# Transposed q copied apart by ScalarE in a retention kernel with a matmul MLP, and another order of its first loads

## The chip, the cores and the metric

The kernel runs on one core of a Trainium2 chip. The metric is the device time of one execution in microseconds (us); lower is better. The kernel before the change took 300.82 us, the median of three runs (300.07, 300.82 and 302.81).

TensorE does the matmuls. VectorE, ScalarE and GpSimd do elementwise work. GpSimd and SyncE also issue the DMA transfers that bring data in and out. Each engine works through its own list of instructions in the order in which the program was written for it; between engines there are only waits on semaphores.

## The reference

```python
# q, k, v: (8 batches, 8 heads, 576 positions, 64); float32
scores = scale * q @ k^T                        # scale = 1/8
Dmat   = gamma[h] ** (i - j) where i >= j else 0
att    = (scores * Dmat) @ v
x      = att.transpose(0, 2, 1, 3).reshape(4608, 512)
h      = x @ w_in                               # w_in: 512 x 2048
out    = 0.5 * h * (1 + erf(h / sqrt(2))) @ w_out   # w_out: 2048 x 512
```

It is an attention with a decay that depends on the head in place of a softmax, and a two-layer MLP with exact GELU over the 4608 tokens that come out of it.

## The kernel before

**Units.** A unit is 128 positions of one batch with all eight heads (or the last 64 positions of two batches, a short unit). Two batches go together as a pair `bp`. Units are collected in groups: groups 0 to 3 are single units, groups 4 to 7 are three pairs and a short unit that TensorE transposes, and groups 8 and up (`BY_DVE`) are 11 pairs and 3 short units. Four units make a block of 512 tokens; the nine blocks go through the MLP one after another.

**Per group.** q and k are loaded (L266 to L317), transposed so that the head dimension lies on partitions, and multiplied to scores (`scores`, L441). VectorE multiplies by the decay mask (`masked`, L490). `inner` (L525) multiplies by v, `state` (L550) makes the 64x64 sum of k times v that later chunks need, and `cross` (L596) adds what q takes from the state of the chunk before it. `evacuate` writes the x tile for the MLP.

**Groups from 8 on.** VectorE transposes 32x32 blocks of 4-byte words (L432). Such a word is a pair of neighbouring bf16 values of the head dimension, so the two numbers of a pair, `y` = 0 and 1, stay side by side in the result. `scores` and `cross` run once for `y` = 0 and once for `y` = 1: for each of four pairs of heads and each `y` four matmuls of 32 rows run in four bands of rows of the array, which is 32 matmuls for a group (L464, L615). q is the operand that streams through. For a pair of units its tokens are read by `turned_q` as (b, u, t) while they lie in memory as (u, b, t, y): two tokens 4 bytes apart, then a jump of 256 bytes to the other half, and back. For a short unit it is an even step of 4 bytes. k is the weight, read with an even step of 4 bytes (`turned_k`).

**MLP.** Block 0 and 1 and blocks 2 to 5 use plain matmuls for the first layer (L658). The last three use a seven-product scheme (`mlp1_fast`, L867), and the second layer uses such a scheme almost throughout (`mlp2_fast`, L762). ScalarE does GELU (L663, L666, L872).

**Who decides the order.** The kernel is one Python loop (L1112 on) that keeps an estimate of every engine's time (`T`), of the landing of loads (`land`) and of free PSUM banks, and writes down next what by those estimates can go next. This is a plan made while the program is built. An entry that a time in the plan delays is only written later into its engine's list; on the chip nothing waits for that time. `fire` (L1045) writes GpSimd's loads in the order of the string `ORDER` (L322), SyncE's loads of v (`load_v`, L257) and the output stores (`put`, L1072).

**Loads.** GpSimd's loads convert to bf16 while they copy. SyncE loads v for the groups from 8 on as float32 in four buffers with the tag `v32`; two of these hold constants at first (`zeros`, `far`), two are free from the start. q and k of a group share one tile with the tag `qk` (four buffers).

Of the kernel before, what the change touches and what calls it, by code (L numbers as in the profile page):

```python
# [17 lines left out]
def kernel(  # L18
# [51 lines left out]
    N_LD = 4  # L70
    N_QKT = 4
# [6 lines left out]
    RATE = 3.8  # L78
    STATE10 = 24.0
# [54 lines left out]
    near = ld_pool.tile([128, 2, HP, 128], FP32, tag="qk", bufs=N_LD, name="near")  # L134
# [21 lines left out]
    def constants():  # L156
# [7 lines left out]
        for h in range(H):  # L164
            nc.scalar.activation(near[:, h % 2, h // 2], far[:, 0, :], AF.Exp, scale=log_gamma[h], bias=ln_scale)
# [64 lines left out]
    def qk_tile(name):  # L230
        return ld_pool.tile([128, 4 * H * D], BF16, tag="qk", bufs=N_LD, name=name)

# [3 lines left out]
    def tiles_of(i):  # L236
        g = groups[group_of[i]]
        if i not in loaded:
            if i < 4:
                loaded[i] = (early_slice(2 * i, 2).rearrange("p (a h d) -> p a h d", a=2, h=H),  # L240
                             early_slice(8 + i, 1).rearrange("p (h d) -> p h d", h=H), None)
            else:
                n = group_of[i]
                if i != g[0]:
                    qk, kn = loaded[i - 1][0], loaded[i - 1][2]
                elif n not in BY_DVE:
                    qk = qk_tile("qk_ld").rearrange("p (a h j d) -> p a h j d", a=2, h=H, j=2)
                    kn = qk[:, 1]
                else:
                    qk = qk_tile("qkb_ld").rearrange("p (a f) -> p a f", a=2)  # L250
                    kn = ld_pool.tile([128, H, 2, D], BF16, tag="kn", bufs=N_KN, name="kn_ld") if len(g) > 1 else None
                loaded[i] = (qk, None if group_of[i] in BY_DVE else ld_pool.tile([128, H, D], BF16, tag="v", bufs=8, name="v_ld"), kn)
        return loaded[i]

    v32 = {}

    def load_v(i):  # L257
# [5 lines left out]
        sw[0] = max(sw[0], T["pe"]) + 0.8  # L263
        land["v", i] = max(T["pe"] + 3.5, sw[0] + 2.0)

    def load(what, i):  # L266
# [25 lines left out]
        if what in "qk" and group_of[i] in BY_DVE:  # L292
# [3 lines left out]
            for jj in (j,) if j is not None else range(2):  # L296
                for e in range(2):
                    p0 = 64 * e + 32 * jj
                    nc.gpsimd.dma_start(qk[p0:p0 + 32, "qk".index(what), 0:HP * per].rearrange("p (h x) -> p h x", h=HP),  # L299
# [10 lines left out]
        for jj in (j,) if j is not None else range(2):  # L310
# [3 lines left out]
            else:  # L314
                dst = qk[:, "qk".index(what)] if i < 4 else qk[0:n, "qk".index(what), :, jj]
# [5 lines left out]
    cast_due = {("q", 0): (loaded[0][0][:, 0], first["q32"]), ("k", 0): (loaded[0][0][:, 1], first["k32"])}  # L321
    ORDER = ("wi0 io k1 q1 v0 k2 wi1 q2 v1 v2 q3 wi4 k3 wi2 v3 wi6 wo0 wi7 wo2 wi3 wi5 wo3 wo1 wo6 wo4 wo5 wo7 k4 "  # L322
             "q5 q4 k5 q6 v4 k6 v5 q7 k7 q8 k8 q9 v7 v8 v6 k9 v9 dq2 q10 dq3 q11 k12 q12 k10 n11 k11 dq4 v10 n12 "
# [70 lines left out]
    def qkT_of(n):  # L394
        s = sg[n]
        if "qkT" not in s:
            if n < 4:
                s["qkT"] = ld_pool.tile([128, 2, HP, 128], BF16, tag="kn", bufs=N_KN, name="qkT")
            else:
                s["qkT"] = tr_pool.tile([128, 2, H, 128], BF16, tag="qkT", bufs=N_QKT, name="qkT")  # L400
        return s["qkT"]

    def turn(n, jj, half):
        qk, qkT = loaded[groups[n][0]][0], qkT_of(n)
        b, t = bank([128, HP, 128], BF16, "qk_ps")
        rows = TAIL if units[groups[n][0]][2] is None else C
        for x in range(HP):
            what = qk[:, jj, 2 * x:2 * x + 2, :] if n < 4 else qk[0:rows, jj, HP * half + x, :, :]
            nc.tensor.transpose(t[:, x, 0:rows], what, ident[0:rows, 0, 0:rows])
        done = pe(0.225)  # L410
        done = either(0.42, 0.6, done, qkT[:, jj, HP * half:HP * half + HP, 0:rows], t[:, :, 0:rows])
# [3 lines left out]
    def turned(n, x):  # L415


        us = 1 if units[groups[n][0]][2] is None else 2
        t = qkT_of(n)[:, x].rearrange("p h s -> p (h s)")[:, 0:HP * us * 128]
        return us, t.rearrange("p (h u b t y) -> p h u b t y", h=HP, u=us, t=2, y=2)  # L420

    def turn_dve(n, x):

        us, t = turned(n, x)
        m = HP * us * 64
        src = loaded[groups[n][0]][0][:, x, 0:2 * m].bitcast(FP32).rearrange("p (h t e) -> p h t e", h=HP, e=32)
        dst = qkT_of(n)[:, x].rearrange("p h s -> p (h s)")[:, 0:2 * m].bitcast(FP32)
        if us == 1 or x == 0:
            src, dst = src.rearrange("p h (u t) e -> p (h u) t e", u=us), dst.rearrange("p (h b t) -> p h t b", t=2, b=32)
        else:  # L430
            src, dst = src.rearrange("p h (t u) e -> p h t u e", u=us), dst.rearrange("p (h u b t) -> p h t u b", h=HP, t=2, b=32)
        nc.vector.transpose(dst, src)  # L432
        sg[n]["T"] = on("dve", 0.13 + m / 960, max(land["qk"[x], i] for i in groups[n])) + SEM

    def turned_q(n, sl, hp, y):
        return turned(n, 0)[1][sl, hp, :, :, :, y].rearrange("p u b t -> p b u t")

    def turned_k(n, sl, hp, y):
        return turned(n, 1)[1][sl, hp, :, :, :, y].rearrange("p u b t -> p (u b t)")

    def scores(n):  # L441
        g = groups[n]
        qkT = sg[n]["qkT"]
        if n < 4:
            got = [bank([128, HP, 128], FP32, "sc") for _ in range(2)]
            for hp in range(HP):
                for e in range(2):
                    sl = slice(64 * e, 64 * e + 64)
                    nc.tensor.matmul(got[e][1][:, hp, :], lhsT=qkT[sl, 1, hp, :], rhs=qkT[sl, 0, hp, :],
                                     start=True, stop=True)  # L450
            st[g[0]]["sc"] = got, pe(0.23, "row")
        elif n in BY_DVE:
# [13 lines left out]
            done = pe(0.27 if short else 0.5, "row4x2" if short else "row4")  # L466
            for j, i in enumerate(g):
                st[i]["sc"] = got if short else got[j], done
        elif len(g) == 1:
            got = [bank([128, H, TAIL], FP32, "sc") for _ in range(2)]  # L470
            for h in range(H):
                for j in range(2):
                    sl = slice(64 * j, 64 * j + 64)
                    nc.tensor.matmul(got[j][1][sl, h, :], lhsT=qkT[sl, 1, h, :TAIL], rhs=qkT[sl, 0, h, :TAIL],
                                     start=True, stop=True)
            st[g[0]]["sc"] = got, pe(0.23, "quad")
        else:
            got = [[bank([128, HP, 128], FP32, "sc") for _ in range(2)] for _ in g]
            for h in range(H):
                for j in range(2):  # L480
                    sl = slice(64 * j, 64 * j + 64)
                    nc.tensor.matmul(got[j][h % 2][1][:, h // 2, :], lhsT=qkT[sl, 1, h, :], rhs=qkT[sl, 0, h, :],
# [7 lines left out]
    def masked(i):  # L490
# [8 lines left out]
        for e in range(2):  # L499
# [6 lines left out]
            else:  # L506
                r = ret_pool.tile([128, HP, 128], BF16, tag=f"ret{e}", name=f"ret{e}")
                by = near[:, e] if i in raw else (mskp if group_of[i] in BY_DVE else msk).to_broadcast([128, HP, 128])
# [41 lines left out]
    def state(bp, ci):  # L550
        pair = pair_of[bp, ci]
        b, u_ps = bank([128, H, D], FP32, "u_ps")
        for hp in range(HP) if packed(pair[0]) else ():
            for y in range(2):
                for e in range(2):
                    for j, i in enumerate(pair):
                        h, p0 = 2 * hp + e, 64 * e + 32 * j
                        keys = loaded[i][0][:, 1, h, y::2] if i < 4 else loaded[i][2][:, h, j, y::2]
# [676 lines left out]
```

## Time and profile before

| | us |
|---|---|
| median of three runs | 300.82 (300.07 to 302.81) |
| the profiled execution | 299.79 |
| its span, first to last instruction | 298.0 |
| TensorE busy | 286.5 |
| VectorE busy | 230.0 |
| GpSimd busy | 152.1 |
| ScalarE busy | 134.3 |

The granted TensorE clock was 1.000 over the span. The profiled execution is 1.79 us longer than its span and 1.03 us shorter than the median. In a line of the profile a group is named by the source line, the engine, the operation and the tiles it writes and reads; the number after `x` counts instructions. Matmuls overlap in the pipeline, and each record lasts until its modelled end, so the time that a run of matmuls costs is read from its start to the start of what follows, not from its busy time. A few per cent of matmul records are missing.

### The profile page before, as it was taken

To read this page: it belongs to the slowest core of one execution; us is meant where nothing else is said; L and a number is where in the kernel's file an instruction comes from. 1 tells how busy PE (TensorE), PEld (TensorE's weight loads), DVE (VectorE), ACT (ScalarE), POOL (GpSimd) and SP (SyncE) were. 2 spreads that over 40 slices of the span, in tenths; PEclk is the share of its full clock that TensorE was granted. 3 is DMA by queue.
4 is the path that set the end of the run, shared out by engine and by line. 5 is a ranking of instruction groups with operands and counts; after the bars stand their busy time and mean duration, and the time that the engine had idled before them with its cause. 6 is when DMAs were issued, how large, how long until landed. Compare 5 with 4: busy or idle time off the path is not lost.

```text
span 298.0 us, 8850 instructions
## 1 busy us (share of the span) xinstructions
PE 286.5 (96%) x3717; PEld 216.2 (73%) x3741; DVE 230.0 (77%) x443; ACT 134.3 (45%) x260; POOL 152.1 (51%) x232
## 2 busy tenths in 40 slices
PE   7999997989999999999999999999999999999994
PEld 2578586868756667666666666666888888888883
DVE  5871795899989899425976789756998999899761
ACT  7456234545254243544342433533554554546521
POOL 8976689879866998999998933000000000000000
PEclk9999999999999999999999999999999999999999
DMA  9999999999999999999999861201102101201013
GB/s 143 167 189 202 184 186 180 194 159 105 143 169 154 169 164 184 147 102 167 216 151 190 72 175 34 70 2 37 37 0 74 70 2 70 73 0 73 35 55 124
DMA packets 112119, 34.79 MB, mean 117 GB/s; under 512 B 89808, under 2 KB 107728, under 8 KB 112080
## 3 DMA queue, kind: packets, MB, share of 16 engines
q0 software_dynamic: 78048, 17.71, 66.8%
q1 hardware_dynamic: 32992, 16.26, 20.7%
q8 instruction: 29, 0.48, 0.7%
q10 hardware_dynamic: 1040, 0.26, 0.4%
q14 instruction: 10, 0.08, 0.1%
HBM read 42.47 MB, written 9.44 MB: 174 GB/s over the span
## 4 chain that ended last, share of the span: by engine, by line
PE 46%; POOL 24%; DMA 21%; issue 4%; DVE 3%; ACT 1%; POOLq 0%
PE fa L762 13%; POOL qkb_ld L299 12%; PE fb L762 10%; DMA kn_ld<-in_k_dram 9%; PE hT L658 7%; PE ha L867 7%; DMA qk_ld<-in_k_dram 6%; PE hb L867 5%; POOL kn_ld L306 5%; DMA w_in<-in_moe_w_in_dram 3%; POOL early L316 3%; DMA v_ld<-in_v_dram 2%; POOL w_in L271 2%; PE o_ps L615 1%; DVE s L730 1%
## 5 line engine op out<-in xcount | busy, mean ns | idle before, releaser
L658 PE MATMUL hT<-x,w_in 128*128 128x512 bf16 (+2 forms) x522 | 92.2, 314 | 1.9 <-ACT x L377 0.4
L658 PEld LDWEIGHTS <-w_in 128*128 128x128 bf16 x544 | 49.4, 98 | 25.0 <-issue 1.9
L762 PEld LDWEIGHTS <-g_all 128*128 128x128 bf16 x544 | 52.4, 98 | 11.8 <-issue 1.1
L663 ACT ACTIVATE g_all<-hT 128x512 bf16<-128x512 f32 x64 | 38.2, 597 | 46.6 <-PE hT L658 44.0
L762 PEld LDWEIGHTS <-s 128*128 128x128 bf16 x408 | 39.4, 98 | 8.9 <-DVE s L730 0.7
L748 DVE TENSOR_TENSOR o_sb<-fb,t 128x256 f32<-128x256 f32 x51 | 21.2, 417 | 22.9 <-PE fb L762 10.0
L872 ACT ACTIVATE g_all<-tt 128x512 bf16<-128x512 f32 x36 | 22.6, 630 | 29.4 <-DVE tt L880 29.3
L762 PE MATMUL fa<-w_out,g_all 128*128 128x256 bf16 x272 | 35.1, 273 | 0.0
L299 POOL DMA_DIRECT2D qkb_ld<-in_k_dram x56 | 30.5, 569 | 5.4 <-DMA kn_ld<-in_k_dram 4.6
L299 POOL DMA_DIRECT2D qkb_ld<-in_q_dram x56 | 30.9, 575 | 4.1 <-DVE ret L509 2.2
L306 POOL DMA_DIRECT2D kn_ld<-in_k_dram x44 | 30.3, 716 | 4.3 <-DMA qkb_ld<-in_q_dram 1.9
L509 DVE TENSOR_TENSOR ret<-sc,mskp 128x512 bf16<-128x512 f32 x44 | 27.2, 677 | 3.0 <-PE sc L464 3.0
L880 DVE TENSOR_TENSOR tt<-hb,tt 128x512 f32<-128x512 f32 x36 | 24.5, 687 | 5.2 <-ACT tt L377 2.9
L377 ACT COPY t<-fa 128x256 f32<-128x256 f32 x38 | 14.1, 372 | 30.4 <-PE fa L762 30.4
L666 ACT ACTIVATE g_all<-hT 128x512 bf16<-128x512 f32 (+1 forms) x36 | 19.3, 552 | 12.5 <-PE hT L658 12.5
L638 DVE TENSOR_TENSOR x<-o_ps,dqT 128x512 bf16<-128x512 f32 (+1 forms) x36 | 20.9, 620 | 1.5 <-PE o_ps L615 1.3
L867 PEld LDWEIGHTS <-ws 128*128 128x128 bf16 x192 | 18.8, 98 | 2.2
L762 PE MATMUL fa<-wt,s 128*128 128x256 bf16 x136 | 17.5, 273 | 0.2 <-DVE s L730 0.2
L762 PE MATMUL fa<-wt,g_all 128*128 128x256 bf16 x136 | 17.5, 273 | 0.2 <-ACT t L377 0.2
L762 PE MATMUL fb<-w_out,g_all 128*128 128x256 bf16 x136 | 17.6, 273 | 0.0
L762 PE MATMUL fb<-wt,s 128*128 128x256 bf16 x136 | 17.5, 273 | 0.0
L762 PE MATMUL fb<-w_out,s 128*128 128x256 bf16 x136 | 17.5, 273 | 0.0
(122 smaller groups left out, 436.3 us busy)
## 6 DMA issues: line engine op xcount, KB each, us to landing
out_dram<-o_sb SPq DMA_DIRECT2D x31, 256.0 KB, 2.3
v<-in_v_dram SPq DMA_DIRECT2D x50, 128.0 KB, 5.5
qkb_ld<-in_q_dram POOLq DMA_DIRECT2D x44, 64.0 KB, 4.0
qkb_ld<-in_k_dram POOLq DMA_DIRECT2D x44, 64.0 KB, 4.3
kn_ld<-in_k_dram POOLq DMA_DIRECT2D x44, 64.0 KB, 4.1
w_in<-in_moe_w_in_dram POOLq DMA_DIRECT2D x8, 256.0 KB, 6.7
w_out<-in_moe_w_out_dram POOLq DMA_DIRECT2D x8, 256.0 KB, 9.8
out_dram<-o_sb SPq DMA_DIRECT2D x8, 128.0 KB, 2.3
```

The costliest lines, as they stand in the source:

```text
L299: nc.gpsimd.dma_start(qk[p0:p0 + 32, "qk".index(what), 0:HP * per].rearrange("p (h x) -> p h x", h=HP), {"q": q, "k": k}[what][2 * bp + jj ...
L306: nc.gpsimd.dma_start(kn[64 * e:64 * e + 64, :, j], k[2 * bp + j, :, ci * C + e:ci * C + C:2, :].rearrange("h s d -> s h d"))
L509: nc.vector.tensor_tensor(r, t, by, op=ALU.mult)
L638: nc.vector.tensor_tensor(x[:, :, n * y:n * y + n], o, dqT[:, :, ci * C:ci * C + n], op=ALU.mult)
L658: nc.tensor.matmul(hT[:, m - m0, :], lhsT=w_in[:, cc, m * 128:m * 128 + 128], rhs=x_tiles[t][:, cc, lo:hi], start=(cc == 0), stop=(cc == N ...
L663: nc.scalar.activation(g_all[:, t % 2, :, m0, :], hT.rearrange("p n (a c) -> p (n a) c", a=2), AF.Gelu)
L666: nc.scalar.activation(g_of(t, 2 * lo // TOK)[:, m0:m0 + n, lo_:lo_ + hi - lo], hT, AF.Gelu)
L748: nc.vector.tensor_tensor(dst, src, f[key], op=ALU.add)
L762: nc.tensor.matmul(dst, lhsT=x[:, kk, :], rhs=y[:, kk, :], start=(name in "125" and kk == 0), stop=(kk == HK - 1), skip_group_check=True)
L867: nc.tensor.matmul(dst[:, m, :], lhsT=a[:, cc, c0:c0 + 128], rhs=y[:, cc, :], start=(name in "125" and m == 0 and cc == 0), stop=(cc == HC ...
L872: nc.scalar.activation(g_of(t, part)[:, m0:m0 + 2], src, AF.Gelu)
L880: nc.vector.tensor_tensor(f[key], f["b"][1], f[key], op=ALU.add)
```

## The change

1. **q apart.** VectorE still transposes q as 4-byte pairs, now into a tile `pairs`, with the tokens in their natural order. A new ScalarE copy (`apart`) then writes the two halves of the pairs, first all `y` = 0 and then all `y` = 1, back into the tile that q was loaded into. `turned_q` becomes a contiguous slice of it. k is left as it was.
2. **Tiles.** q and k have tiles of their own: six for q (`lq`), four for k (`lk`). The q tile is now in use until `cross` has read it. Temporaries and sums of the seven-product scheme move to these tiles; their number and work stay.
3. **Plan.** Durations assumed for scores and cross are shorter. A new `share` adds the cost of SyncE's transfers to the estimated landings of others. Stores of block 0 are written no earlier than a planned 60 us (`STORE_AT`), loads of v no earlier than a planned 58 us (`V_AT`).
4. **Order.** `ORDER` is another string.

```diff
+    N_LQ = 6
+    N_LK = 4
+    N_TQ = 2
+    N_TK = 4
+    STORE_AT = 60.0
+    V_AT = 58.0
+    CROWD = 66.0
...
-    ORDER = ("wi0 io k1 q1 v0 k2 wi1 q2 v1 v2 q3 wi4 k3 wi2 v3 wi6 wo0 wi7 wo2 wi3 wi5 wo3 wo1 wo6 wo4 wo5 wo7 k4 "
-             "q5 q4 k5 q6 v4 k6 v5 q7 k7 q8 k8 q9 v7 v8 v6 k9 v9 dq2 q10 dq3 q11 k12 q12 k10 n11 k11 dq4 v10 n12 "
+    ORDER = ("wi0 io k1 v1 q1 k3 v0 q2 k2 q3 wi1 v2 wi5 wi7 v3 wo4 wi6 wi4 wi2 wo2 wo1 wi3 wo0 wo3 wo7 wo5 wo6 k4 "
+             "q4 q5 k5 v4 k6 q6 v5 q7 k7 v8 q8 dq2 k8 q9 v6 v7 k9 v9 dq3 q11 k12 q10 q12 k10 n11 dq4 k11 n12 v10 "
...
+    def apart():
+        n, ready = apart_due.pop(0)
+        m = pairs_of(n)
+        nc.scalar.copy(loaded[groups[n][0]][0][0][:, 0:2 * m].rearrange("p (y n) -> p y n", y=2),
+                       sg[n]["pairs"].rearrange("p h s -> p (h s)")[:, 0:2 * m].rearrange("p (n y) -> p y n", y=2))
+        sg[n]["T"] = max(sg[n].get("T", 0.0), on("act", 0.15 + m / 580, ready) + SEM)
...
     def turned_q(n, sl, hp, y):
-        return turned(n, 0)[1][sl, hp, :, :, :, y].rearrange("p u b t -> p b u t")
+        m = pairs_of(n)
+        return loaded[groups[n][0]][0][0][sl, y * m + hp * m // HP:y * m + (hp + 1) * m // HP]
...
-        while v_due and v_due[0] < nV + N_V32 and v_due[0] <= nA + V_LEAD and ("q", v_due[0]) in land:
+        while v_due and now > V_AT and v_due[0] < nV + N_V32 and v_due[0] <= nA + V_LEAD and ("q", v_due[0]) in land:
             load_v(v_due.pop(0))
...
+        while apart_due and apart_due[0][1] <= now + 0.1 and T["act"] <= now + (0.5 if apart_due[0][0] > group_of[min(nA, N_U - 1)] else 3.0):
+            apart()
...
-        while stores and stores[0][0] <= now + 0.2:
+        while stores and max(stores[0][0], STORE_AT if stores[0][1] == 0 else 0.0) <= now + 0.2:
             put()
```

In the built programs SyncE's list begins so (the numbers in names tell buffers apart; each `v` entry is two loads of 128 KB):

```
before: load q, 4 stores of block 0, then v 1041, 1203, 1251, 1383, 1532, 1550, 2 stores, ...
after:  load q, v 1192, 1195, then 4 stores of block 0, then v 1245, 1493, 1514, 1532, 2 stores, ...
```

The loads of v 1192 and 1195 wait for no semaphore. GpSimd's list has the same instructions in another order. TensorE's list has two more warming matmuls (23 in place of 21), and ScalarE's has 14 more copies: 11 of 128x1024 and 3 of 128x512 elements.

## The prediction

> **What bounds the kernel.** I read the stages first.
>
> ```profile
> 0.00:15.00 15.00, 13.24 (x110) 5.97 (x112) 10.54 (x43) 9.15 (x22) 13.86 (x22) 1.00 1.63 155
> 15.00:36.00 21.00, 20.52 (x237) 15.85 (x237) 10.51 (x22) 11.24 (x23) 14.33 (x19) 1.00 1.52 193
> 36.00:66.00 30.00, 27.02 (x421) 22.02 (x420) 25.13 (x45) 13.80 (x27) 25.60 (x37) 1.00 2.01 181
> 66.00:120.00 54.00, 53.51 (x875) 37.30 (x880) 50.37 (x91) 21.94 (x41) 44.64 (x77) 1.00 1.24 154
> 120.00:205.00 85.00, 83.30 (x1277) 56.37 (x1291) 56.32 (x103) 34.60 (x66) 53.65 (x81) 1.00 0.78 115
> 205.00:294.00 89.00, 88.91 (x807) 78.72 (x805) 76.75 (x145) 43.61 (x81) 0.00 (x0) 1.00 0.14 47
> ```
>
> Columns: stage, length, busy us of TensorE, its weight loads, VectorE, ScalarE, GpSimd, then clock, DMA share and GB/s. From 66 to 294 us TensorE is busy 225.7 of 228 us, so a microsecond less of matmul there comes off the end. The chain of waits runs over loads up to about 145 us, but TensorE has other work queued meanwhile. Only before 66 us does it stand still for data; the timeline shows where, and how long blocks of small matmuls take.
>
> ```profile
> 49.08 0.61 PE L409 MATMUL qk_ps<-ident,qk_ld 128*128 128x128 bf16 x8 [1.49 <-DMA qk_ld<-in_q_dram]
> ...
> 51.36 0.62 PE L482 MATMUL sc<-qkT 64*128 64x128 bf16 x16
> 51.92 2.79 PE L658 MATMUL hT<-x,w_in 128*128 128x256 bf16 x24
> ...
> 57.35 0.62 PE L482 MATMUL sc<-qkT 64*128 64x128 bf16 x16
> 57.81 0.28 PE L409 MATMUL qk_ps<-ident,qk_ld 64*128 64x64 bf16 x4
> ...
> 62.28 0.39 PE L409 MATMUL qk_ps<-ident,qk_ld 64*128 64x64 bf16 x8 [1.47 <-DMA qk_ld<-in_k_dram]
> ...
> 158.14 0.42 PE L559 MATMUL u_ps<-vh,kn_ld 128*32 128x64 bf16 x32
> 158.49 0.85 PE L615 MATMUL o_ps<-qkT,u_sb 32*64 32x128 bf16 x32
> 159.27 0.84 PE L464 MATMUL sc<-qkT 32*128 32x128 bf16 x32
> 160.04 1.05 PE L762 MATMUL fb<-w_out,g_all 128*128 128x256 bf16 x8
> ```
>
> From start to start cross (L615) takes 0.78 us and scores (L464) 0.77: eight steps of four parallel matmuls over 128 tokens, and the single starts lie 84 ns apart. L482 also makes eight steps over 128 tokens (two parallel matmuls each), but reads q contiguously: 0.56 us, starts 56 ns apart.
>
> **The contiguous q.** There are 11 full score blocks and 9 full cross blocks (352/32 and 288/32 in the groups). At L482's 0.56 each saves 0.22: 20 x 0.22 = 4.4 us. That the jumps cause the 84 ns, and not the four bands, is read from the short blocks: same four bands, 64 tokens in an even step of 4 bytes, 32 ns per step; twice that is 64, not 84. It also gives the low bound, since k as weight keeps its 4-byte step: 64 ns a step saves 8 x 20 ns = 0.16 a block, 3.2 us in all. High bound: 0.46, the L482 block at 57.35 that runs straight into the next, 0.32 x 20 = 6.4. I take 4.4, because L482 is followed by the same change of mode. The six short blocks take 0.38; 32 contiguous matmuls of 64 columns take 0.35 (158.14 to 158.49): 6 x 0.03 = 0.2. Sum **-4.6** (-3.4 to -6.6).
>
> [...]
>
> **ScalarE's copies.** They are new, in a list that GELU shares.
>
> ```profile
> L377 ACT COPY t<-fa 128x256 f32<-128x256 f32 x38 | 14.1, 372 | 30.4 <-PE fa L762 30.4
> L377 ACT COPY tt<-ha 128x512 f32<-128x512 f32 x17 | 9.6, 579 | 3.3 <-PE ha L867 3.2
> L576 ACT CAST u_sb<-u_acc 128x512 bf16<-128x512 f32 x8 | 4.9, 618 | 13.4 <-DVE u_acc L574 13.4
> ```
>
> From 256 to 512 elements a copy grows by 0.21 us; 1024 then take 0.58 + 2 x 0.21 = 1.0, which is an estimate from these rows. Eleven of these and three of 512 make 12.7 us. Between 66 and 205 us ScalarE works 56.5 of 139 us, so they fit. Behind a copy in the list stand GELUs and PSUM evacuations, and TensorE waits for those through its eight banks. The cover is shown by L576: eight times ScalarE stood, 13.4 us in all, for VectorE, while the idle time of TensorE that its copies to u_acc (L571) ended is 0.4 us in the group of L658. I put **+0.4** (0 to 12.7). VectorE's 28 transposes keep count and size (694 and 424 ns): 0. So do the w_in sums (681 ns each) and the seven products: 0. The q tile is held until cross, but there are six of them and the load of a sixth-next group is written only after the state of an earlier one: 0; without that cover GpSimd would stand behind a full q tile for up to a group, some 9 us, late loads that TensorE would meet.
>
> **SyncE.** What holds v and the stores back is a time in the plan; the chip sees only the list.
>
> ```profile
> 38.59 12.79 SPq L1076 DMA_DIRECT2D out_dram<-o_sb  x4
> 51.42 27.14 SPq L262 DMA_DIRECT2D v<-in_v_dram  x12
> ```
>
> Before, the first loads of v stood behind stores that waited for their data, and left at 51.42. Afterwards four of them stand ahead of those stores and wait for nothing: they leave from about 1.2 us on, 0.63 us apart. The stores leave when their data are there, as before. So 512 KB move from 51 us into the head. What that costs others is bounded by the loads' latencies with and without v beside them:
>
> ```profile
> v<-in_v_dram SPq DMA_DIRECT2D x8, 128.0 KB, 6.9
> qkb_ld<-in_k_dram POOLq DMA_DIRECT2D x4, 64.0 KB, 6.4
> ...
> qkb_ld<-in_k_dram POOLq DMA_DIRECT2D x8, 64.0 KB, 3.0
> ```
>
> The first two lines are from 50 to 60 us, the third from 64 to 76. Eight v loads add 3.4 us to a load; four would add 1.7, and the plain packet time of four (2048 packets of 20.5 ns over 16 engines) is 2.6. The nearest undisturbed case is 0, since in the head loads land 5.0 to 5.6 us after issue without growing, so the DMA is not yet backed up there. I take **+1.0** (0 to 2.6).
>
> **GpSimd's first loads.** The new order puts units 1 to 3 ahead of the second slice of w_in. The last q that TensorE then needs before steady MLP work is GpSimd's ninth load, issued at about 8.9 us (nine steps of 0.9) and landing at 14.2; transposes, state and scores (0.2, 0.35, 0.33) bring the first hT to about 15.2. Before, hT came at 14.84, with one slice done earlier, unit 3's transposes still to do, and a stall of 0.42 at 18.5. That cancels: 0. Two more warming matmuls fall into waits: 0, at most 0.4 if the wait is gone. Later the two waits, 1.49 and 1.47, remain in question. Up to 60 us eight v loads go out either way, so k of unit 10, the second of the two, lands near 62 again, unless the head had spare bandwidth, which brings it up to 2.6 us earlier. TensorE has 8 hT matmuls (0.9 us) less to do ahead of it than before. I take **-0.8** for both (-3.0 to +1.7, the high end being 0.9 of work put off and 0.8 for the later q9, which now has two entries more before it).
>
> **Sum.** -4.6 + 0.4 + 1.0 - 0.8 = -4.0: the profiled execution 299.79 becomes 295.8, its span 294.0. That execution was 1.03 below the median, so I forecast **296.8 us**.
>
> **Rivals.** About 1% (3 us) is what a measurement can tell from no change.
> - *The hold-back does the reverse.* The four v loads delay the head by the full 2.6 and neither wait shrinks: -4.6 + 0.4 + 2.6 = -1.6, 299.2. For it: no semaphore on them. Against: latencies in the head are flat.
> - *Both waits go.* Their 3.0 us vanish and the head stays: -4.6 + 0.4 - 3.0 = -7.2, 293.6. For it: earlier v loads and better spread transposes; against: the same bytes before 60 us.
> - *Reading is not the limit.* Blocks stay at 0.78, because two tokens side by side already hide the jump and four bands or k's weight loads set the 84 ns. Then +0.4 + 1.0 - 0.8 = +0.6, 301.4. For it: both full blocks, with unlike weights, take the same 84. Against: 32 ns in the short blocks. [...]
> - *Slower: the copies block GELU.* The place is ScalarE's list from 66 to 120 us, where VectorE is busy 50.4 of 54 us, so transposes come late, the copy waits for them and all GELUs behind it. If two thirds of 12.7 are uncovered (8.5), -4.4 + 8.5 = +4.1, 304.9. It is slower from 4.4 us uncovered on, by over 1% from 7.4, or 0.53 a copy. For it: VectorE at 93%; against: the 13.4 us of L576 that cost nothing.
>
> **Chances.** Forecast 0.50 (own range 294.8 to 298.8), reverse 0.18, both waits go 0.15, no gain 0.08, slower 0.09. Faster by over 1% (under 297.8): 0.40 of the forecast's, 0.15, and 0.02 of the reverse case, 0.57. Slower by over 1%: 0.08 of the last and 0.01 of the no-gain case, 0.09. Within 1%: 0.34. The range 293.0 to 301.0 takes in the first three cases and half of the fourth; it leaves out the slower one and tails.
>
> **What would show it.** Full score and cross blocks near 0.56 from start to start; if they stay at 0.78, the main step is wrong. Copies of 1024 near 1.0 us; a gap on TensorE released by ScalarE behind them would be the slower rival. SyncE's first v loads at about 1 to 4 us, and the first early k landing later than 7.8 us, would show the reverse. The waits at 47 and 60 us gone, or moved, settles the third term.

## The result, and the profile after

| | before | after |
|---|---|---|
| median, us | 300.44 (4 runs, 299.28 to 302.81) | 305.25 (4 runs, 303.37 to 306.79) |
| the profiled execution, us | 299.79 | 305.13 |
| its span, us | 298.0 | 303.4 |
| granted clock over the span | 1.000 | 0.989 |

The change makes the kernel slower by 1.5%: the ratio is 1.0151, with an interval of 1.0106 to 1.0196. The forecast was 296.8 us, a gain. The four runs of before here include the three of the prediction.

The stages of the kernel after come first. The columns are those of the table by stage in the prediction.

```profile
0.00:15.00 15.00, 11.27 (x63) 4.27 (x65) 7.92 (x39) 8.19 (x20) 12.85 (x21) 1.00 1.95 157
15.00:36.00 21.00, 20.95 (x276) 16.60 (x275) 11.18 (x22) 12.66 (x25) 13.26 (x18) 1.00 1.46 196
36.00:66.00 30.00, 26.41 (x346) 19.88 (x345) 24.27 (x44) 12.49 (x25) 25.65 (x35) 0.97 2.04 174
66.00:120.00 54.00, 52.16 (x877) 36.78 (x881) 47.27 (x83) 27.24 (x47) 48.80 (x85) 0.98 1.28 157
120.00:205.00 85.00, 81.09 (x1252) 54.46 (x1265) 65.54 (x110) 40.34 (x73) 52.56 (x77) 0.98 0.79 115
```

From 66 to 205 us TensorE is now busy 133.25 us, against 136.81 before (53.51 + 83.30): in the same 139 us it stands still 3.6 us more, and the clock is 0.98 there. The head is emptier too, 11.27 us against 13.24. The last stretch, the seven-product scheme, runs as before; it starts at 213.60 us instead of 208.21, and that 5.4 us is the whole difference of the spans. Over the whole span TensorE is busy about as long as before (286.1 against 286.5 us) and idle 5.8 us longer.

Next is the timeline of TensorE in the kernel after: start, duration, line, tiles, and in brackets the idle time before it and what ended it.

```profile
8.59 1.60 PE L1126 MATMUL warm<-zeros 128*128 128x512 bf16 x4
11.91 0.62 PE L436 MATMUL qk_ps<-ident,early 128*128 128x128 bf16 x8 [1.72 <-DMA early<-in_q_dram]
...
17.65 1.91 PE L702 MATMUL hT<-x,w_in 128*128 128x256 bf16 x16
...
60.75 1.36 PE L702 MATMUL hT<-x,w_in 128*128 128x256 bf16 x11
64.47 0.58 PE L436 MATMUL qk_ps<-ident,qk_ld 64*128 64x64 bf16 x8 [2.35 <-DMA qk_ld<-in_k_dram]
64.98 3.26 PE L702 MATMUL hT<-x,w_in 128*128 128x256 bf16 x16
...
75.81 0.63 PE L508 MATMUL sc<-q_ld,kT 32*128 32x128 bf16 x32
76.37 1.05 PE L806 MATMUL fa<-w_out,g_all 128*128 128x256 bf16 x8
...
82.13 0.64 PE L659 MATMUL o_ps<-q_ld,u_sb 32*64 32x128 bf16 x32
82.70 1.05 PE L806 MATMUL fa<-wt,g_all 128*128 128x256 bf16 x8
```

Three things are to be seen. The full blocks are as fast as forecast: scores (L508) take 0.56 us from start to start, cross (L659) 0.57. The head has a new gap of 1.72 us, in which TensorE waits for an early q. And the wait for k of unit 10, 1.47 us at 62 before, is 2.35 us at 64; the 16 matmuls behind it take 3.26 us where 24 such took 2.79 before, since they run at half the clock, a granted 0.50. That half clock holds from 64.35 to 67.77 us, and again from 180.40 to 183.81, behind a wait of 2.24 us at 180. Each costs about 1.7 us, so the shorter blocks took some 4 us off TensorE's busy time and the half clock put 3.4 us back.

The idle time from 66 to 205 us has a few places. This one is at 116 us; first TensorE, then ScalarE, both from the timeline of the kernel after.

```profile
115.37 1.03 PE L702 MATMUL hT<-x,w_in 128*128 128x512 bf16 x3
117.67 1.03 PE L806 MATMUL fa<-wt,s 128*128 128x256 bf16 x8 [1.27 <-ACT t L398]
```

```profile
115.81 0.59 ACT L615 COPY u_acc<-u_ps 128x512 f32<-128x512 f32 x1 [2.41 <-DVE u_sb L613]
116.29 1.05 ACT L472 COPY q_ld<-qT 128x1024 bf16<-128x1024 bf16 x1
117.24 0.38 ACT L398 COPY t<-fa 128x256 f32<-128x256 f32 x1
```

TensorE waits for `t`, which frees its bank. In ScalarE's list the new copy of q (L472) stands just ahead of it and takes 1.05 us; the entry before that had waited 2.41 us for VectorE. This is the slower rival of the prediction in one picture: the copy delays an evacuation that TensorE needs, and about 1.0 of the 1.27 us is its doing. The price of the copies in the groups is as estimated:

```profile
L472 ACT COPY q_ld<-qT 128x1024 bf16<-128x1024 bf16 x11 | 11.4, 1039 | 0.0
L472 ACT COPY q_ld<-qT 128x512 bf16<-128x512 bf16 x3 | 1.8, 614 | 0.0
```

What was not foreseen is VectorE's part. With the tokens in their natural order its full transposes of q take 1093 ns in place of 694; those of k stay near 700. The first line is of before, where q and k are one group, the others of after:

```profile
L432 DVE STREAM_TRANSPOSE qkT<-qkb_ld 128x512 f32<-128x512 f32 x22 | 14.9, 694 | 0.0
```

```profile
L461 DVE STREAM_TRANSPOSE qT<-q_ld 128x512 f32<-128x512 f32 x11 | 12.0, 1093 | 0.0
L461 DVE STREAM_TRANSPOSE kT<-k_ld 128x512 f32<-128x512 f32 x11 | 7.8, 705 | 0.0
```

### The profile page after: what moved, and what is told of

Its sections match the earlier page's. It is cut to its first block, busy times and chain, and to the rows that moved or that the text cites. A ratio compares the mean times of both kernels' runs of the same rounds, so it can differ in the third digit from the quotient of the medians.

```text
span 303.4 us, 8920 instructions
## 1 busy us (share of the span) xinstructions
PE 286.1 (94%) x3719; PEld 214.2 (71%) x3743; DVE 235.8 (78%) x443; ACT 146.7 (48%) x274; POOL 153.1 (50%) x232
## 5 line engine op out<-in xcount | busy, mean ns | idle before, releaser
L702 PE MATMUL hT<-x,w_in 128*128 128x256 bf16 (+2 forms) x522 | 93.5, 320 | 1.4 <-DVE x L682 0.3
L915 ACT ACTIVATE g_all<-t 128x512 bf16<-128x512 f32 x36 | 22.6, 630 | 29.4 <-DVE t L923 29.3
L320 POOL DMA_DIRECT2D q_ld<-in_q_dram x56 | 31.2, 585 | 3.3 <-DMA k_ld<-in_k_dram 1.4
L320 POOL DMA_DIRECT2D k_ld<-in_k_dram x56 | 30.7, 570 | 2.8 <-DMA kn_ld<-in_k_dram 1.5
L923 DVE TENSOR_TENSOR t<-hb,t 128x512 f32<-128x512 f32 x36 | 24.5, 688 | 5.1 <-ACT t L398 2.8
L806 PE MATMUL fb<-w_out,g_all 128*128 128x256 bf16 x136 | 18.3, 280 | 2.2 <-DVE x L682 2.2
L562 POOL TENSOR_TENSOR vh<-v,dvp 128x512 bf16<-128x512 f32 x14 | 15.4, 1130 | 6.1 <-PE u_ps L603 5.0
L774 DVE TENSOR_TENSOR s<-g_all 128x1024 bf16<-128x1024 bf16 x17 | 12.0, 704 | 8.4 <-ACT g_all L710 7.3
```

The source lines that it names most:

```text
L320: nc.gpsimd.dma_start(qk["qk".index(what)][p0:p0 + 32, 0:HP * per].rearrange("p (h x) -> p h x", h=HP), {"q": q, "k": k}[what][2 * bp + jj ...
L702: nc.tensor.matmul(hT[:, m - m0, :], lhsT=w_in[:, cc, m * 128:m * 128 + 128], rhs=x_tiles[t][:, cc, lo:hi], start=(cc == 0), stop=(cc == N ...
L806: nc.tensor.matmul(dst, lhsT=x[:, kk, :], rhs=y[:, kk, :], start=(name in "125" and kk == 0), stop=(kk == HK - 1), skip_group_check=True)
L915: nc.scalar.activation(g_of(t, part)[:, m0:m0 + 2], src, AF.Gelu)
L923: nc.vector.tensor_tensor(f[key], f["b"][1], f[key], op=ALU.add)
```

## The experiments

Medians taken at different times stand against different runs of before, so each experiment is read by its ratio to the kernel before on the same chip. 0.0033 is 1 us. Names of kernels are labels.

**The v loads alone, late and in front.** `e_v_late` is the kernel after with SyncE's first four v loads behind block 0's four stores; `e_v_front` is the kernel before with those four at the head of SyncE's list. All other lists are unchanged in both.

```diff
 e_v_late (on after)
-            nc.sync.dma_start(v32[i][64 * e:64 * e + 64], src.rearrange("h s d -> s h d"))
+            held_v.append((v32[i][64 * e:64 * e + 64], src.rearrange("h s d -> s h d")))
...
+        if t == 0 and not any(x[1] == 0 for x in stores) and len(stored0) == 3:
+            issue_v()
```

```diff
 e_v_front (on before)
+    for i in v_due[:2]:
+        load_v(i)
```

> The changed kernel with one thing moved: SyncE's four loads of v that stood at the head of its list stand behind the four stores of block 0, as in the kernel before. All other lists are the same, instruction for instruction. Theory A (those four loads, not held back but sent first, cost the head and by it the rest): first steady MLP matmuls at about 15.2 us in place of 17.65, the 1.7 us wait for q at 11.9 gone, the time 2 to 4 us lower, 301 to 303. Theory B (the new order of GpSimd's loads and of TensorE's list costs it, whoever sends v first): the time within 1 us of the changed kernel's, 304 to 306.

> The kernel before with one thing moved: SyncE's first four loads of v stand at the head of its list. All other lists are the same. Theory A: the same cost as in the changed kernel, a wait for q or k of unit 1 of 1 to 2 us near 9 to 11 us, the time 1.5 to 3 us higher, 302 to 304. Theory B: within 1 us of the kernel before.

Measured: `e_v_late` 303.0 us, ratio 1.0120 (1.0062 to 1.0178); `e_v_front` 303.21 us, ratio 1.0119 (1.0082 to 1.0156). The first two fences are the DMA issues in the first 20 us of the kernel before and of `e_v_front` (KB each, median us from issue to landing), then comes the timeline of TensorE in `e_v_front`, then one line of the kernel before.

```profile
early<-in_v_dram POOLq DMA_DIRECT2D x4, 128.0 KB, 5.6
early<-in_k_dram POOLq DMA_DIRECT2D x3, 128.0 KB, 5.2
early<-in_q_dram POOLq DMA_DIRECT2D x3, 128.0 KB, 5.5
```

```profile
v<-in_v_dram SPq DMA_DIRECT2D x4, 128.0 KB, 6.6
early<-in_v_dram POOLq DMA_DIRECT2D x4, 128.0 KB, 8.5
...
early<-in_k_dram POOLq DMA_DIRECT2D x3, 128.0 KB, 7.7
early<-in_q_dram POOLq DMA_DIRECT2D x3, 128.0 KB, 8.3
```

```profile
8.11 1.03 PE L1087 MATMUL warm<-zeros 128*128 128x512 bf16 x2
11.87 1.03 PE L413 MATMUL qk_ps<-ident,early 128*128 128x128 bf16 x8 [2.73 <-DMA early<-in_q_dram]
...
17.44 0.94 PE L662 MATMUL hT<-x,w_in 128*128 128x128 bf16 x8
```

```profile
17.52 0.61 PE L658 MATMUL hT<-x,w_in 128*128 128x128 bf16 x8
```

Four v loads ahead make the early loads take 2.5 to 2.9 us longer from issue to landing, and TensorE stands 2.73 us for the first of them. There is a second cost: the record of the granted clock shows full speed from 18.11 us on, in the kernel before from 9.10 on. (The clock of 1.000 given for these kernels leaves this first stretch out.) So at 17.44 us eight small matmuls take 0.94 us, where they take 0.61 in the kernel before. The first oT of block 0 comes at 37.07 us instead of 31.30. Of these 5.8 us about 3 come back, because both waits at 47 and 60 us are gone from the trace; 2.9 us are left between the two profiled spans, 3.6 by the ratio.

In the kernel after the four loads cost the head 2.2 us (the first oT at 33.41 against 31.25 in `e_v_late`), but the ratios of the two, 1.0151 and 1.0120, are only 0.9 us apart and their intervals overlap. The trace of `e_v_late` shows where some of the gain goes: TensorE comes to the wait for k of unit 10 earlier and stands there longer, 3.25 us against 2.35.

```profile
57.72 1.92 PE L710 MATMUL hT<-x,w_in 128*128 128x256 bf16 x16
62.88 0.39 PE L444 MATMUL qk_ps<-ident,qk_ld 64*128 64x64 bf16 x8 [3.25 <-DMA qk_ld<-in_k_dram]
```

**The copies alone, with two plans.** `e_apart_only` is the kernel after with the old `ORDER`, no hold-back and the old estimate of SyncE's transfers. `e_apart_same_plan` goes further: all entries of TensorE, GpSimd and SyncE stand in the order of the kernel before, and only the 14 copies, the transposes' pattern and the tiles of their own for q and k are added.

```diff
 e_apart_only (on after)
-    STORE_AT = 60.0
-    V_AT = 58.0
+    STORE_AT = 0.0
+    V_AT = 0.0
...
-        land["v", i] = share(T["pe"], 0.8) + 0.6
+        sw[0] = max(sw[0], T["pe"]) + 0.8
+        land["v", i] = max(T["pe"] + 3.5, sw[0] + 2.0)
...
+    ORDER = ("wi0 io k1 q1 v0 k2 wi1 q2 v1 v2 q3 wi4 k3 wi2 v3 wi6 wo0 wi7 wo2 wi3 wi5 wo3 wo1 wo6 wo4 wo5 wo7 k4 "
```

> The changed kernel with the old ORDER, no held stores or loads of v and the old estimate of SyncE's cost: what is left of the change is q copied apart, its tiles and the plan's shorter durations. Theory A and B both: the blocks at 0.56 us give their 4.3 us and the head is that of the kernel before, 296 to 298. A third theory (the 14 copies in ScalarE's list shift the plan so that TensorE waits between 66 and 205 us): 300 or more, with TensorE's waits of over 1 us there as in the changed kernel (116, 160 and 178 us).

> The kernel before with q copied apart and nothing else: TensorE's, GpSimd's and SyncE's lists are those of the kernel before, VectorE's differs in how the transposes write, ScalarE's has the 14 copies more. Theory C (the copies and the shorter blocks are a gain, and what took it back in the run with q apart alone is the other plan, which lets TensorE meet loads of code, VectorE and buffers at worse places): waits after 66 us about as before, 2 to 3 us in all, the time 296 to 298. Theory D (the copies themselves, in ScalarE's list, make TensorE wait as much as the blocks save): 299.5 to 302, with waits that ScalarE ends.

Measured: `e_apart_only` 300.92 us, ratio 1.0018 (0.9984 to 1.0052); `e_apart_same_plan` 302.6 us, ratio 1.0082 (1.0047 to 1.0116). Nothing is gained, though the blocks have the fast form in both. The longest group of waits of TensorE in `e_apart_same_plan` (us in total, times, longest), their places in its timeline, and what VectorE and ScalarE did before the first of them:

```profile
PE sc L511 <- ACT q_ld L474: 3.2, 3, 1.5
```

```profile
80.86 0.63 PE L511 MATMUL sc<-q_ld,kT 32*128 32x128 bf16 x32 [0.94 <-ACT q_ld L474]
...
108.79 0.63 PE L511 MATMUL sc<-q_ld,kT 32*128 32x128 bf16 x32 [1.50 <-ACT q_ld L474]
...
118.08 0.63 PE L511 MATMUL sc<-q_ld,kT 32*128 32x128 bf16 x32 [0.74 <-ACT q_ld L474]
```

```profile
76.07 1.11 DVE L464 STREAM_TRANSPOSE qT<-q_ld 128x512 f32<-128x512 f32 x1
```

```profile
79.24 0.62 ACT L623 CAST u_sb<-u_acc 128x512 bf16<-128x512 f32 x1 [2.25 <-DVE u_acc L621]
79.77 1.04 ACT L474 COPY q_ld<-qT 128x1024 bf16<-128x1024 bf16 x1
```

q was transposed at 77.18 us, but its copy started at 79.77: in ScalarE's list it stands behind a cast that waited 2.25 us for VectorE. At 108 us the copy likewise stands behind an entry that waited for VectorE (1.18 us) and starts 1.7 us after q was transposed; at 118 us it stands behind a GELU. The 3.2 us are these three. With the plan of `e_apart_only` no scores wait for a copy, but the time comes back elsewhere: 2.3 us for `u_acc` (ScalarE), 0.7 for `s` (VectorE) and 1.6 us in the middle of a cross block with no releaser shown. No copy of q stands ahead of that `u_acc`; ScalarE had itself waited 2.65 us for VectorE there. So in that kernel the loss is not shown to be the copies'.

**The contiguous read without copies.** In `e_pairs_even`, on the kernel before, VectorE writes q's tokens in natural order, and TensorE reads them in an even step of 4 bytes, as k's. There are no copies, and all lists are as before.

```diff
 e_pairs_even (on before)
-            src, dst = src.rearrange("p h (u t) e -> p (h u) t e", u=us), dst.rearrange("p (h b t) -> p h t b", t=2, b=32)
+            dst = dst.rearrange("p (h b t) -> p h t b", h=HP, b=32)
...
-        return turned(n, 0)[1][sl, hp, :, :, :, y].rearrange("p u b t -> p b u t")
+        us, t = turned(n, 0)
+        return qkT_of(n)[sl, 0].rearrange("p h s -> p (h s)")[:, hp * us * 128 + y:(hp + 1) * us * 128:2]
```

> The kernel before with the transposes of q writing the tokens in natural order, and TensorE reading q in an even step of 4 bytes: no copies, all five lists as before. If jumps and not the 4-byte step made the blocks slow: steps of 64 ns, full blocks at 0.60 to 0.64 us, and the time 297 to 298.5. If the 4-byte step is the cause: blocks at 0.78 still and the time within 1 us of before.

Measured: 297.79 us over 10 runs, ratio 0.9919 (0.9890 to 0.9948): faster than both kernels. Its timeline:

```profile
80.74 0.64 PE L465 MATMUL sc<-qkT 32*128 32x128 bf16 x32
81.31 6.22 PE L659 MATMUL hT<-x,w_in 128*128 128x512 bf16 x28
...
88.38 0.65 PE L616 MATMUL o_ps<-qkT,u_sb 32*64 32x128 bf16 x32
88.96 0.64 PE L465 MATMUL sc<-qkT 32*128 32x128 bf16 x32
```

0.57 and 0.58 us from start to start, against 0.56 and 0.57 with contiguous q. The even step gives nearly all of the shorter blocks (20 blocks, 4.0 us in all); the two halves didn't have to be taken apart. The time fell by 2.4 us only. VectorE's full transposes of q are as slow here as in the kernel after (the 22 of q and k take 904 ns in the mean, 694 before); whether they take the other 1.6 us no run tells. And as this kernel and `e_apart_same_plan` have the same lists but for the copies, were run side by side, and read q almost equally fast, the copies cost 302.60 - 297.79 = 4.8 us there. Part of it is the clock: among the runs with a granted clock of 0.998 or more (four and six) the difference of the means is 3.7 us, near the 3.2 us of waits.

**The loads alone.** `e_loads_only` is the kernel before with the new `ORDER`, the hold-back and the new estimate; q is read as before.

```diff
 e_loads_only (on before)
+    ORDER = ("wi0 io k1 v1 q1 k3 v0 q2 k2 q3 wi1 v2 wi5 wi7 v3 wo4 wi6 wi4 wi2 wo2 wo1 wi3 wo0 wo3 wo7 wo5 wo6 k4 "
...
+        while v_due and now > V_AT and v_due[0] < nV + N_V32 and v_due[0] <= nA + V_LEAD and ("q", v_due[0]) in land:
...
+        while stores and max(stores[0][0], STORE_AT if stores[0][1] == 0 else 0.0) <= now + 0.2:
```

> The kernel before with the new ORDER, the held stores and loads of v and the new estimate of SyncE's cost, but with q read in pairs as before and no copies. Theory A and B: it pays the head and the waits without the gain of the blocks, 304 to 309, and the granted clock below 1 wherever TensorE stands over 2 us. The third theory: 301 to 303, as the waits after 66 us are the copies' doing.

Measured: 305.34 us, ratio 1.0168 (1.0130 to 1.0207). The loads alone are as slow as the whole change. Its trace has a gap of 2.96 us in the head, 1.7 us for k of unit 10, and half clock from 12.1 and from 186.2 us on.

**Filling the wait.** `e_fill` is the kernel after with 12 matmuls of no use ahead of the transposes of k of unit 10, meant to keep TensorE busy while it waits, and the clock from dropping there.

```diff
 e_fill (on after)
+        if n == 7 and jj == 1 and half == 0:
...
+            for _ in range(12):
+                nc.tensor.matmul(t, lhsT=w_in[:, 0, 0:128], rhs=w_in[:, 0, 0:512], start=True, stop=True)
```

> The changed kernel with 12 matmuls of no use (128x512, 2.6 us) ahead of the transposes of k of unit 10, where TensorE waits 2.4 us for a load; all else the same. If a wait of that length is what halves TensorE's clock for 3.4 us afterwards, the stretch of half clock at 64 us is gone, one stretch (near 180) stays, and the time is 1 to 2 us lower, 303 to 304.5. If it is something else, both stretches stay and the time is that of the changed kernel, 304.5 to 306.

Measured: 306.72 us, ratio 1.0214 (1.0148 to 1.0281), no gain. There is no half clock at 64 us in its trace, but one at 12.8 (behind a gap of 2.23 us in the head) and one at 190.3 (behind a wait of 2.46 us). The drops of the clock are not bound to one place, and taking one away says little.

**k of unit 10 earlier.** In the new `ORDER` that load stands behind q of 11 and 12 and k of 12, as it does in the old one; in both, 51 entries stand ahead of it. Here it is written three loads earlier. The planner then also rewrites parts of the other lists.

```diff
 e_v_late_k10 (on e_v_late)
-             "q4 q5 k5 v4 k6 q6 v5 q7 k7 v8 q8 dq2 k8 q9 v6 v7 k9 v9 dq3 q11 k12 q10 q12 k10 n11 dq4 k11 n12 v10 "
+             "q4 q5 k5 v4 k6 q6 v5 q7 k7 v8 q8 dq2 k8 q9 v6 v7 k9 v9 dq3 q10 k10 q11 k12 q12 n11 dq4 k11 n12 v10 "
```

> The kernel after with the four v loads late (303.0 us), and k of unit 10 written three loads (q and k of units 11 and 12) earlier into GpSimd's list. The planner then also writes parts of the other lists in another order. Theory E (the new order of loads costs its 2 us over the kernel with only the copies, 300.9, by the wait of 3.4 us for k of unit 10): that wait shrinks to 1.7 us or less, no other load ends a wait over 1 us before 66 us, the first 64x64 scores of TensorE's own transposes move from 66.1 to about 64.5, and the time is 301 to 301.5. Rival F (the bytes up to 60 us set when TensorE goes on, whatever their order): another load ends a wait of about 3 us between 55 and 66 us and the time stays within 1 us of 303.0. Rival G (what differs is the plan after 66 us, each written order having its own waits of VectorE's, ScalarE's and the issue kind): the first 60 us gain what E says and the time does not follow.

> The kernel before with q read evenly from the pairs (297.8 us), and k of unit 10 written three loads earlier; the planner rewrites parts of the lists here too. In that kernel the waits for loads before 66 us were 1.8 us (q at 47) and no wait for k of unit 10. Theory E: no wait to remove, so 297.8 within 1. Rival G: a new plan has its own waits after 66 us, and the time can go either way by up to 2 us (295.8 to 299.8); the sum of the waits over 0.3 us after 66 us, 9 in 297.8's trace with 9 us in all, tells.

Measured: `e_v_late_k10` 305.26 us, ratio 1.0218 (1.0177 to 1.0259). It wasn't the experiment that was meant: in its new plan six v loads stood at the head of SyncE's list again. Its trace shows it, with a gap of 3.43 us in the head, half clock for 6.8 us behind it, and the first hT at 21.48 us. `e_even_k10` (the same move on `e_pairs_even`) 300.29 us, ratio 1.0053 (1.0013 to 1.0092), over `e_pairs_even` by 2.5 us in the medians and 4.0 in the ratios, which no wait in its trace explains: the trace, with a span of 296.5 us, is that of its fastest run. (Of `e_pairs_even` the expectation names nine waits over 0.3 us behind 66 us, 9 us in all; its timeline shows five, 4.6 us in all.) So the v loads were held as they should be in `e_late_k10b`, with all other lists those of `e_v_late_k10`:

```diff
 e_late_k10b (on e_v_late_k10)
-        if i > v_first[1]:
+        if stored_all:
             issue_v()
```

> The kernel of e_v_late_k10 with all its first v loads behind block 0's four stores; there six of them had still stood at the head of SyncE's list, so that run had two edits in it. All other lists are those of e_v_late_k10. The head: the gap of 3.43 us at 9.6 and the half clock behind it go, the first hT comes near 15.0 instead of 21.48, the first oT near 31.3 instead of 37.21, as in e_v_late. Theory E (the new order's 2 us are the wait for k of unit 10, 3.4 us in e_v_late): with k of unit 10 earlier the sum of the waits for loads from 40 to 66 us is under 3 us against 4.8 in e_v_late, and the time is 300 to 301.5. Rival F (bytes, not order): the waits for loads in that stretch still sum to 4 us or more and the time is 302 to 304. Rival G (the waits after 66 us belong to each written order): the loads wait less but the time stays at 302 to 304 because the waits of over 0.3 us after 66 us sum to more than the 6 us of e_v_late.

Measured: 303.29 us, four runs from 299.4 to 305.61, ratio 1.0118 (1.0029 to 1.0207): too wide to decide. Both kernels were run again, side by side on one chip.

> The same kernel as e_v_late, on one chip with e_late_again, for a closer interval. Both theories: 303.0 within 1, with the wait of 3.4 us for k of unit 10.

> The same kernel as e_late_k10b, whose four runs lay between 299.4 and 305.6 us. Theory E (the new order's 2 us are the wait for k of unit 10): 1.5 us or more under e_v_late_again. Rival G (the waits after 66 us belong to each written order and take the gain back): within 1 us of e_v_late_again, with more waits over 0.3 us after 66 us than its 6.2 us.

Measured: `e_v_late_again` 304.36 us (6 runs), ratio 1.0126 (1.0081 to 1.0171); `e_late_again` 300.79 us (12 runs), ratio 1.0003 (0.9972 to 1.0035). This load three entries earlier, with the plan that follows from it, is worth 3.6 us here. The timeline of TensorE in `e_v_late_again`, then in `e_late_again`:

```profile
57.85 1.92 PE L710 MATMUL hT<-x,w_in 128*128 128x256 bf16 x16
61.59 0.39 PE L444 MATMUL qk_ps<-ident,qk_ld 64*128 64x64 bf16 x8 [1.82 <-DMA qk_ld<-in_k_dram]
```

```profile
56.02 0.39 PE L445 MATMUL qk_ps<-ident,qk_ld 64*128 64x64 bf16 x8
56.73 0.27 PE L445 MATMUL qk_ps<-ident,qk_ld 64*128 64x64 bf16 x4 [0.32 <-DVE x L691]
57.33 0.27 PE L445 MATMUL qk_ps<-ident,qk_ld 64*128 64x64 bf16 x4 [0.32 <-DVE x L691]
```

The wait for the load is gone there; 0.6 us for VectorE is in its place. The profiled waits over 0.3 us behind 66 us are alike (4.6 us and 4.4 us). The two profiled executions are only 1.3 us apart in span, the one of `e_v_late_again` being its fastest run, so that the part of the 3.6 us that lies in the wait itself (1.8 us here, 3.25 in `e_v_late`) is shown, and the rest is not located. The planner moved other entries too, and a rewritten plan alone can weigh as much: in `e_even_k10` the same move cost 2.5 to 4.0 us, where TensorE had not waited for that load at all. So the 3.6 us are not shown to be this load's.

## Why the prediction was wrong

The measured ratios add up step by step, in us of 300.44: the copies and the contiguous read together +0.5 (`e_apart_only`), the new order with v late +3.2 more (the mean of `e_v_late` and its repeat, 1.0123), the v loads in front +0.8 more (1.0151): 4.5 us. The forecast was -4.0. Each step has an interval of one to two us; by the medians of the two, which were run side by side, the new order costs 2.1, not 3.2. Two steps of the prediction failed by some 4 us each: the cover of ScalarE's copies (+0.4 put, 3 to 5 measured), and the two terms of the loads (+1.0 and -0.8 put, +4.0 measured by this sum and +5.0 in `e_loads_only`).

**The contiguous q: right.** -4.4 was forecast for the full blocks; 11 x (0.77 - 0.56) + 9 x (0.78 - 0.57) is 4.2. The short blocks stayed at 0.38, so the further 0.2 didn't come. That jumps in the reading set the 84 ns, and not the four bands or k, is confirmed by two forms of q that don't jump: 0.56 and 0.57. With them the rival in which reading is not the limit has fallen. The low bound was too careful as well: it doubled the 32 ns of a step in the short blocks to 64, but with the even step the single starts lie 57 ns apart (56 with contiguous q). Why the jumps cost 28 ns a step (84 against 56) no run here shows.

**ScalarE's copies: the cover failed.** The size was right, 13.2 us against 12.7, and 1.04 us a copy. The cover wasn't: "I put +0.4" rested on L576, whose casts had waited 13.4 us for VectorE without TensorE noticing. But that idle time was no free room. A copy that stands behind such a cast waits with it, as at 80 us in `e_apart_same_plan`. And the consumer of `u_sb` is the cross of a later chunk, while scores use q next, and the evacuations of `t` behind a copy free banks that TensorE needs next. So the slack of one group of ScalarE said nothing of the slack of another entry. Measured with the lists of before: 4.8 us against `e_pairs_even`. That is near the slower rival's mechanism, with 4.8 of 13.2 us uncovered instead of 8.5, just over its point of decision of 4.4. With the planner free to move things `e_apart_only` is 3.0 us over `e_pairs_even` by the ratios, and 4.7 us over what the blocks' 4.2 us should give; how much of that is the copies' stays open.

**VectorE's transposes: a term put at nothing.** "VectorE's 28 transposes keep count and size: 0" took the durations of before for those of after. The 11 full transposes of q grew by 0.40 us each, 4.4 us in all, on the engine for which the copies' neighbours in ScalarE's list wait. What this costs TensorE by itself no run shows.

**SyncE's v loads: the mechanism right, the size of the delay too small.** They left at 1.24 to 3.37 us, as said, and the first early k landed at 9.47 instead of 7.82. The head was delayed by 2.2 us in the kernel after and by 5.8 us in the kernel before, where +1.0 was taken because latencies in the head didn't grow. They didn't grow at the load of before; with 512 KB more they grew from 5.2 to 5.6 up to 7.2 to 7.4 us (7.7 to 8.5 in `e_v_front`). So the flat 5.2 to 5.6 us of before had not shown that there was room for 512 KB. Of the 2.2 us about 0.8 were left at the end by the ratios; the wait for k of unit 10, 0.9 us shorter than in `e_v_late`, took up a part.

**GpSimd's first loads and the two waits: wrong in sign.** -0.8 became +3.2 by the ratios. The step that failed is the overlap, how much work TensorE has ahead of k of unit 10. In `e_v_late` that load was issued at 55.79 us, 0.4 us later than before, and landed at 62.75, so "lands near 62 again" held. But TensorE stood for it from 59.63 us on instead of 60.81, and the wait grew from 1.47 to 3.25 us. The prediction had seen that TensorE has 0.9 us less to do there, and had put it only at the high end of its range. In the kernel after, with the v loads in front, the load was issued at 58.28 and landed at 64.33 us, and TensorE waited 1.0 and 2.35 us. Together the waits for loads from 40 to 66 us are 4.1 us in `e_v_late` against 2.5 in `e_apart_only`; the rest of the 3.2 is not located. `e_late_again` is free of it when the load stands earlier, in another plan.

**Not in any term: the clock.** Half clock (a granted 0.50) came twice in the trace of after, 6.8 us in all; in the trace of before, once the head had reached full speed, only behind its last instruction. In the trace of after it came behind waits of 2.35 and 2.24 us, so these two were dearer than they look, by about 1.7 us each; the sums above hold it, since they are made from whole runs.

What stays open is a wait with no releaser in the middle of a block of small matmuls, mostly near 160 us. Its longest is 0.8 to 2.7 us in all new kernels but `e_even_k10` (0.3), also in `e_loads_only` and `e_pairs_even`, which have no copies; the profiled execution of before has 0.2 us at 100 us and no more. It differs by execution: 1.16 us in `e_v_late`, 2.34 in `e_v_late_again`, the same kernel. All 15 such waits over 0.3 us ended 2.4 to 3.0 us after a transfer of the queue q8 began, which the profile lists as instructions (some 17 from 66 to 205 us); in the kernel after one began at 158.38 and the wait ended at 160.74 us. So TensorE may have waited for its own instructions; no run was made to tell.

## What to carry to other kernels

Slack has to be read for the entry that comes behind the new one on its engine, and for who needs that entry next; another group's idle time on the same engine is no cover. When a load's place in a list changes, follow that one load from its issue to the first instruction that needs it, and don't only sum bytes. And where two tokens side by side with a jump read slowly, try an even step first: it gave 0.57 us against 0.56 for the contiguous form without a copy. It was not free either: VectorE's full transposes of q took 1.1 us in place of 0.7.

## What was not expected of the hardware

In the trace of after the half clock came in two stretches of 3.41 us, which start at 64.35 and 180.40 us, 116.05 us or 34 such lengths apart; in `e_loads_only` it starts at 12.1 and 186.2, 51 such lengths apart. The length of a wait alone doesn't sort them: the clock dropped around a wait of 1.6 us (`u_acc`, in `e_loads_only`), but not behind the 3.25 us near 60 us in `e_v_late`. The share of idle time sorts the traces of before and after better, with TensorE's idle time counted in steps of 3.41 us from the start of full speed (9.10 and 9.74 us) to the end of TensorE's work. In the trace of after, the two steps ahead of the half clock are idle for 65% (60.94 to 64.35 us, with the wait of 2.35 us) and 67% (176.99 to 180.40 us, with the wait of 2.24 us). Behind a step of 50% (9.74 to 13.15 us, with the wait of 1.72 us) the granted clock stays at 1.00, and so it does in the trace of before behind steps of 44% (the wait of 1.49 us), 43% (1.47 us) and 54% (292.40 to 295.81 us, where TensorE's work ends). Whether the share decides it so few cases don't show.

VectorE's subtractions for the second layer take 0.68 us by themselves. Beside GpSimd's `vh` they took up to 2.56 us; the timeline of VectorE and then of GpSimd in the kernel after:

```profile
174.80 1.12 DVE L774 TENSOR_TENSOR s<-g_all 128x1024 bf16<-128x1024 bf16 x1
175.96 1.43 DVE L774 TENSOR_TENSOR s<-s,g_all 128x1024 bf16<-128x1024 bf16 x1
177.31 2.56 DVE L774 TENSOR_TENSOR g_all<-g_all 128x1024 bf16<-128x1024 bf16 x1
179.79 0.74 DVE L682 TENSOR_TENSOR x<-o_ps,dqT 128x256 bf16<-128x256 f32 x2
```

```profile
175.41 3.91 POOL L562 TENSOR_TENSOR vh<-v,dvp 128x512 bf16<-128x512 f32 x3
```

Three subtractions take 5.1 us in place of 2.0, the three `vh` 3.9 in place of some 3.2, and the x tile behind them ended TensorE's wait of 2.24 us at 180. The trace of before has single cases, up to 1.99 us at 142.6, and cost TensorE 0.2 us there. Why the two engines slow down beside each other is not shown: no run here tried it apart.
